# A head pair's two score matmuls start together, once both of their PSUM banks are free

## The chip, the cores and the metric

One core of one Trainium2 chip runs the whole program. The metric is the device time of one execution in microseconds, the median of several. Engine names are those of the profile: PE is TensorE's matmuls, PEld its weight loads, DVE VectorE, ACT ScalarE, POOL GpSimd, SP SyncE, which issues the DMAs.

## The reference

Sliding-window attention with sink tokens, and after it two feed-forward layers on its output:

```
scores = q @ k.T / sqrt(64);  keep = (key < n_sink) | (0 <= query - key < window)     # 4 sinks, window 128
a = softmax(where(keep, scores, -1e9));  x = a @ v                                    # batch 2, 8 heads, 768 tokens, 64 dims
x = relu(x @ w_in)**2 @ w_out                                                         # 1536 tokens, 512 -> 2048 -> 512
h = x @ w_in2;  out = (P(h) / Q(|h|)) @ w_out2                                        # rational function, P of degree 3, Q of degree 2
```

## The kernel before

**Attention** is cut into 24 steps: batch `bb` (2), block `j` of 256 queries (3), head pair `hp` (4). A step is `attention(bb, j, hp)` (L304). It takes two halves `qb` of 128 queries. In each half, both heads `hd` of the pair have one score matmul into a PSUM tile of their own, named `s{bb}_{j}_{hp}_{qb}{hd}`; in the rows of the order the batch is left out, so `s_2_0_10` is block 2, head pair 0, second half, first head. In batch 0 (`kl is None`) a head's q and k lie in 64 of the 128 partitions, head 0 in rows 0 to 63 and head 1 in rows 64 to 127, and a score is one f32 matmul at L329, which the hardware runs as two records. In batch 1 a head's operands are split into a high and a low part over 128 rows (L331, L332). I call the pair of the first half (`00`, `01`) pair a, and that of the second half (`10`, `11`) pair b.

After the scores, DVE merges the two key blocks under a predicate (L340), adds the mask and takes the row's minimum (L341), ACT takes the exponential (L348), DVE the reciprocal of the sum (L349, L350), POOL scales the row (L352). PE then transposes it into two more tiles, `pt` (L357, read by ACT at L365) and `sx` (L360, last read by DVE at L371), and multiplies with v into a tile `xo` (L382 to L386, last read by DVE at L390).

**The banks.** All these tiles come in turn from one pool of four PSUM banks: `ps_at = ... bufs=4, space=PSUM` (L186). A tile's first matmul waits until the tile that had its bank before has been read. The scheduler gives a tile the bank that comes free first, mostly that of the tile allocated four before. A step takes seven tiles: `s00 s01 s10 s11 pt sx xo`. Three steps are in flight (`att_pieces`, L491): the scores of step t, the transposes of step t-1, the output of step t-2. So four before pair a stand `s11` of step t-1 and `pt` of step t-2, and four before pair b stand `sx` of step t-2 and `xo` of step t-3. Where `xo` is read too late, `s11` takes the bank of its own step's `s00` instead: so in steps (1, 0) and (1, 1) among others.

**Beside it** runs the first feed-forward layer for the finished tokens (L400 into `h`, L439 into `acc`), and the decoding of its weights, which arrive as 64-bit words, in halves of 512 columns: ACT L63 and L65, DVE L66 and L67, ACT L299, POOL L300. The first 16 such halves are done while attention of batch 0 runs.

**The order** of each engine's queue is not that of the code. The framework's scheduler simulates the program and issues what is ready first, engine by engine (`schedule_with_timeline_sim=True`); on the chip every queue then runs strictly in that order.

Of the kernel before, what the change touches and what calls it, by code (L numbers as in the profile page):

```python
# [8 lines left out]
F32 = mybir.dt.float32  # L9
# [5 lines left out]
ALU = mybir.AluOpType  # L15
# [5 lines left out]
P = 128  # L21
# [5 lines left out]
SK = 32  # L27
# [13 lines left out]
def f32(ap):  # L41
    return ap.bitcast(F32)
# [133 lines left out]
def banded(ctx, tc, const, qk0, qk1, vb, vs, ns_f, win_f, wp, ab, scalars, out):  # L176
    nc = tc.nc
# [8 lines left out]
    ps_at = att_ctx.enter_context(tc.tile_pool(name="ps_at", bufs=4, space=PSUM))  # L186
    ps_a2 = att_ctx.enter_context(tc.tile_pool(name="ps_a2", bufs=2, space=PSUM))
    ac = att_ctx.enter_context(tc.tile_pool(name="ac", bufs=1))
    at = att_ctx.enter_context(tc.tile_pool(name="at", bufs=2))
# [4 lines left out]
    xh = [pers.tile([P, 4, 512], F32R, name=f"xh{g}", tag=f"xh{g}") for g in range(3)]  # L194
    xl = [pers.tile([P, 4, 512], F32R, name=f"xl{g}", tag=f"xl{g}") for g in range(3)]
# [105 lines left out]
        wh[L], wl[L] = h, lo  # L301


    def attention(bb, j, hp):  # L304

        n = f"{bb}_{j}_{hp}"
# [5 lines left out]
        e = at.tile([P, 2, 2 * W], F32, tag="e", name=f"e{n}")  # L312
        qk, kl, v = loaded[bb, j, hp]

        for qb in range(2):
            first = j == 0 and qb == 0
            nk = W if first else K0
            ss = []
            for hd in range(2):
                if hd == 0:  # L320
                    off = W * qb if j else 0
                else:
                    off = P if first else (W * (1 - qb) if j else 0)
                s = ps_at.tile([P, 512], F32, tag="at", name=f"s{n}_{qb}{hd}")
                cols = slice(qb * P, (qb + 1) * P)
                if kl is None:

                    rows = slice(hd * D, (hd + 1) * D)
                    nc.tensor.matmul(s[:, :nk], lhsT=qk[rows, cols], rhs=qk[rows, 256 + off : 256 + off + nk], start=True, stop=True)  # L329
                else:  # L330
                    nc.tensor.matmul(s[:, :nk], lhsT=qk[hd][:, cols], rhs=qk[hd][:, 256 + off : 256 + off + nk], start=True, stop=False)  # L331
                    nc.tensor.matmul(s[:, :nk], lhsT=qk[hd][:, cols], rhs=kl[hd][:, off : off + nk], start=False, stop=True)  # L332
                ss.append(s)
            for hd, s in enumerate(ss):
                u = 2 * qb + hd

                lo = 0 if hd == 0 or first else P
                if not first:
                    prev, own = (s[:, 0:P], s[:, W:K0]) if hd == 0 else (s[:, W:K0], s[:, 0:P])
                    nc.vector.copy_predicated(prev, own_u, own)  # L340
                nc.vector.tensor_tensor_reduce(  # L341
                    out=e[:, qb, hd * W : (hd + 1) * W], in0=s[:, lo : lo + W], in1=add[min(2 * j + qb, 2)][:, SK * (1 - hd) : SK * (1 - hd) + W],
                    scale=-SCALE, scalar=3.0e38, op0=ALU.add, op1=ALU.min, accum_out=nm[:, u : u + 1])
            c = slice(2 * qb, 2 * qb + 2)
            for hd in range(2):
                u = 2 * qb + hd
                eu = e[:, qb, hd * W : (hd + 1) * W]
                nc.scalar.activation(eu, eu, AF.Exp, bias=nm[:, u : u + 1], scale=-1.0, accum_out=sm[:, u : u + 1])  # L348
            nc.vector.tensor_scalar(out=rs[:, c], in0=sm[:, c], scalar1=GUARD, scalar2=None, op0=ALU.add)  # L349
            nc.vector.reciprocal(rs[:, c], rs[:, c])  # L350
            eq = e[:, qb, :].rearrange("p (h w) -> p h w", h=2)
            nc.gpsimd.tensor_tensor(out=eq, in0=eq, in1=rs[:, c].unsqueeze(2).to_broadcast([P, 2, W]), op=ALU.mult)  # L352
            yield
        pt = ps_at.tile([P, 4, P], F32, tag="at", name=f"pt{n}")
        for u in range(4):
            c0 = 0 if u < 2 else W + SK
            nc.tensor.matmul(pt[:, u, :], lhsT=e[:, u % 2, c0 : c0 + P], rhs=ident, is_transpose=True, start=True, stop=True)  # L357
        sx = ps_at.tile([P, 256], F32, tag="at", name=f"sx{n}")
        for qb in range(2):
            nc.tensor.matmul(sx[:, qb * P : (qb + 1) * P], lhsT=e[:, qb, P : 2 * P], rhs=ident, is_transpose=True, start=True, stop=True)  # L360

        pT = at.tile([P, 4, 2, P], F32, tag="pT", name=f"pT{n}", bufs=1)
        pa = at.tile([P, 4, P], F32, tag="pa", name=f"pa{n}", bufs=1)
        sT = at.tile([P, 256], F32R, tag="sT", name=f"sT{n}")
        nc.scalar.copy(pa, pt)  # L365
        nc.gpsimd.affine_select(out=pT[:, :, 1, :], in_=pa, pattern=[[0, 4], [1, P]], compare_op=ALU.is_ge, fill=0.0, base=0, channel_multiplier=-1)
        nc.gpsimd.affine_select(out=pT[:, :, 0, :], in_=pa, pattern=[[0, 4], [-1, P]], compare_op=ALU.is_gt, fill=0.0, base=0, channel_multiplier=1)

        half = slice(0, 2 * SK)
        nc.scalar.copy(sT[half], sx[half])  # L370
        nc.vector.tensor_tensor(out=sT[2 * SK :], in0=sx[half], in1=f32(sT[half]), op=ALU.subtract)  # L371
        yield
        xo = ps_at.tile([P, 256], F32, tag="at", name=f"xo{n}")
        pf = pT.rearrange("p (h q) o c -> p h (q o c)", q=2)
        nb = 2 if j == 0 else 3

# [10 lines left out]
        t0 = bb * S + j * 256  # L387
        g, c0 = t0 // 512, t0 % 512
        nc.scalar.copy(xh[g][:, hp, c0 : c0 + 256], xo)
        nc.vector.tensor_tensor(out=xl[g][:, hp, c0 : c0 + 256], in0=xo, in1=f32(xh[g][:, hp, c0 : c0 + 256]), op=ALU.subtract)  # L390
        yield


# [341 lines left out]
```

## Time and profile before

| | us |
|---|---|
| median of three runs | 660.72 (658.3 to 661.92) |
| the profiled execution | 661.41 |
| its span in the profile | 659.7 |
| PE busy | 638.3 (97%) |
| DVE, ACT, POOL busy | 464.2, 459.9, 400.1 |

Attention of batch 0, which the change touches, lies in the first 93 us; that of batch 1 ends before 200 us, and the rest is the feed-forward layers. A busy PE is not a PE at its best: two matmuls that run at the same time count once in its busy time, and at half clock a matmul counts twice as long.

### The profile page before, as it was taken

How to read it: one execution, taken by the hardware profiler on the slowest of the kernel's cores; microseconds unless marked ns; L12 is line 12 of the kernel's file. 1: busy time of each engine (PE TensorE's matmuls, PEld its weight loads, DVE VectorE, ACT ScalarE, POOL GpSimd, SP SyncE). 2: the span in 40 equal slices, each digit the busy share in tenths (PEclk: the TensorE clock that was granted, in tenths of full speed). 3: DMA queues.
4: the chain of work that ended last, by engine and by line, in shares of the span. 5: the costliest groups of instructions: out<-in, count | busy, mean ns of one | idle time of the engine just before them, and what ended most of it. 6: DMA issues, size and time to landing. Idle time of an engine off the chain costs nothing.

```text
span 659.7 us, 10180 instructions
## 1 busy us (share of the span) xinstructions
PE 638.3 (97%) x3376; PEld 523.5 (79%) x3376; DVE 464.2 (70%) x969; ACT 459.9 (70%) x938; POOL 400.1 (61%) x367
## 2 busy tenths in 40 slices
PE   5999999999999999999999999999999999999995
PEld 3567789999999887888888887878888888888883
DVE  7988977888823777737521489976699877676674
ACT  6877867767835767557432699977899776767771
POOL 4868867978735667556452789654666654444441
PEclk9979999999999999999999999999999999999998
DMA  7655553454001435304300042200020000001012
GB/s 246 199 172 166 167 165 94 127 131 128 26 13 38 155 128 178 142 28 163 128 1 0 19 140 66 96 1 0 22 106 33 1 0 1 0 1 64 1 64 70
DMA packets 25725, 54.16 MB, mean 82 GB/s; under 512 B 2880, under 2 KB 11072, under 8 KB 25664
## 3 DMA queue, kind: packets, MB, share of 16 engines
q1 hardware_dynamic: 25664, 53.43, 25.1%
q8 instruction: 29, 0.48, 0.3%
q14 instruction: 32, 0.26, 0.1%
HBM read 50.27 MB, written 3.15 MB: 81 GB/s over the span
## 4 chain that ended last, share of the span: by engine, by line
PE 72%; DVE 13%; ACT 7%; issue 3%; POOL 2%; DMA 1%; SPq 0%; DVEq 0%; ACTq 0%; POOLq 0%
PE h L400 31%; PE acc L441 16%; PE acc L439 15%; DVE wt L67 4%; PE xo L382 3%; DVE wr L66 3%; ACT sign L65 2%; PE s L329 2%; PE pt L357 2%; ACT wt L63 1%; POOL wl L300 1%; PE xo L385 1%; PE s L332 1%; DVE h L171 1%; PE s L331 1%
## 5 line engine op out<-in xcount | busy, mean ns | idle before, releaser
L164 POOL TENSOR_TENSOR z<-z,u 128x512 f32<-128x512 f32 x48 | 63.8, 1329 | 75.2 <-ACT z L163 75.0
L300 POOL TENSOR_TENSOR wl<-wt,wh 128x512 fp32r<-128x512 f32 x64 | 91.2, 1433 | 28.5 <-ACT wh L299 26.0
L409 POOL TENSOR_TENSOR gl<-sq,gh 128x256 fp32r<-128x256 f32 (+1 forms) x66 | 69.6, 1055 | 63.1 <-ACT gh L407 26.9
L409 POOL TENSOR_TENSOR gl<-z,gh 128x512 fp32r<-128x512 f32 x47 | 63.8, 1358 | 30.4 <-ACT gh L407 22.4
L66 DVE SCALAR_TENSOR_TENSOR wr<-wr,sign 128x512 uint32<-128x512 uint32 x64 | 60.3, 942 | 26.7 <-ACT sign L65 26.5
L130 DVE TENSOR_TENSOR sq<-sq,h 128x256 f32<-128x256 f32 (+1 forms) x66 | 35.5, 538 | 57.5 <-ACT sq L128 57.0
L67 DVE SCALAR_TENSOR_TENSOR wt<-wt,wr 128x512 uint32<-128x512 uint32 x64 | 67.4, 1053 | 3.6
L439 PE MATMUL acc<-gh,wh 128*128 128x256 f32 (+1 forms) x264 | 65.0, 334 | 1.2 <-ACT wh L299 1.2
L170 DVE SCALAR_TENSOR_TENSOR z<-z,con,h 128x512 f32<-128x512 f32 x48 | 35.7, 745 | 40.6 <-ACT h L169 36.6
L439 PE MATMUL acc<-gh,wl 128*128 128x256 f32 (+1 forms) x264 | 64.1, 332 | 0.0
L439 PE MATMUL acc<-gl,wh 128*128 128x256 f32 (+1 forms) x264 | 64.1, 335 | 0.0
L400 PE MATMUL h<-xh,wh 128*128 128x256 f32 (+1 forms) x264 | 61.3, 343 | 0.0
L441 PE MATMUL acc<-wh,gh 128*128 128x512 f32 x192 | 60.3, 393 | 0.1
L128 ACT ACTIVATE sq<-h 128x256 f32<-128x256 f32 (+1 forms) x66 | 31.4, 475 | 41.3 <-PE h L400 31.1
L441 PE MATMUL acc<-wl,gh 128*128 128x512 f32 x192 | 59.9, 391 | 0.0
L299 ACT CAST wh<-wt 128x512 fp32r<-128x512 f32 x64 | 39.3, 620 | 28.0 <-DVE wt L67 27.0
L400 PE MATMUL h<-xl,wh 128*128 128x256 f32 (+1 forms) x264 | 58.0, 336 | 0.0
L400 PE MATMUL h<-xh,wl 128*128 128x256 f32 (+1 forms) x264 | 57.4, 337 | 0.0
L441 PE MATMUL acc<-wh,gl 128*128 128x512 f32 x192 | 56.8, 390 | 0.0
L400 PE MATMUL h<-x2h,wh 128*128 128x512 f32 x192 | 53.8, 398 | 2.1 <-DVE z L172 2.1
L400 PE MATMUL h<-x2l,wh 128*128 128x512 f32 x192 | 53.6, 396 | 0.0
L400 PE MATMUL h<-x2h,wl 128*128 128x512 f32 x192 | 53.2, 396 | 0.0
(104 smaller groups left out, 1567.1 us busy)
## 6 DMA issues: line engine op xcount, KB each, us to landing
wr<-in_wp SPq DMA_DIRECT2D x64, 512.0 KB, 3.5
qkr<-in_qk SPq DMA_DIRECT2D x32, 176.0 KB, 3.1
v<-in_vb SPq DMA_DIRECT2D x16, 192.0 KB, 3.2
out<-accsb SPq DMA_DIRECT2D x12, 256.0 KB, 2.1
qkr<-in_qk SPq DMA_DIRECT2D x8, 352.0 KB, 3.9
qkr<-in_qk SPq DMA_DIRECT2D x16, 136.0 KB, 2.9
qkr<-in_qk SPq DMA_DIRECT2D x4, 272.0 KB, 4.9
v<-in_vb SPq DMA_DIRECT2D x8, 128.0 KB, 3.2
```

Source lines behind the costliest of these rows:

```text
L66: nc.vector.scalar_tensor_tensor(out=lo, in0=lo, scalar=29, in1=s, op0=ALU.logical_shift_right, op1=ALU.bitwise_or)
L67: nc.vector.scalar_tensor_tensor(out=t, in0=t, scalar=3, in1=lo, op0=ALU.logical_shift_left, op1=ALU.bitwise_or)
L128: nc.scalar.activation(r, h, AF.Relu)
L130: nc.vector.tensor_tensor(out=r, in0=r, in1=h, op=ALU.mult)
L164: nc.gpsimd.tensor_tensor(out=z, in0=z, in1=u, op=ALU.mult)
L170: nc.vector.scalar_tensor_tensor(out=z, in0=z, scalar=con[:, 2:3], in1=h, op0=ALU.add, op1=ALU.mult)
L299: nc.scalar.copy(h[:, c], t)
L300: nc.gpsimd.tensor_tensor(out=lo[:, c], in0=t, in1=f32(h[:, c]), op=ALU.subtract)
L400: nc.tensor.matmul(h[:, :n], lhsT=w_[:, k * P : (k + 1) * P], rhs=x_[:, k, c0 : c0 + n], start=p_ + k == 0, stop=p_ + k == 5)
L409: eng.tensor_tensor(out=gl[:, :n], in0=y, in1=f32(gh[:, :n]), op=ALU.subtract)
L439: nc.tensor.matmul(acc[m][:, :n], lhsT=w_[:, 512 + m * P : 512 + (m + 1) * P], rhs=g_[:, :n], start=st, stop=sp, skip_group_check=True)
L441: nc.tensor.matmul(acc[m], lhsT=g_[:, m * P : (m + 1) * P], rhs=w_[:, 512:1024], start=st, stop=sp)
```

## The change

In `attention`, both tiles of a half are allocated before its first matmul. A list `readers` notes the last reader of each tile of the pool, in the order of allocation. In batch 0 the first head's score matmul gets an explicit wait for the readers of both banks that the pair will take (the tiles three and four before), and the second head's matmul is tied by `keep_in_program_order` to its place behind the first. In batch 1 nothing is added.

```diff
+        def bank(shape, name):
+            readers.append(None)
+            return ps_at.tile(shape, F32, tag="at", name=name)
 ...
-            ss = []
-            for hd in range(2):
+            first_bank = len(readers)
+            tiles = [bank([P, 512], f"s{n}_{qb}{hd}") for hd in range(2)]
+            for hd, s in enumerate(tiles):
...
-                s = ps_at.tile([P, 512], F32, tag="at", name=f"s{n}_{qb}{hd}")
...
-                    nc.tensor.matmul(s[:, :nk], lhsT=qk[rows, cols], ...)
+                    mm = nc.tensor.matmul(s[:, :nk], lhsT=qk[rows, cols], ...)
+                    if hd:
+                        tc.keep_in_program_order(mm)
+                    elif first_bank >= 4:
+                        for r_ in readers[first_bank - 4 : first_bank - 2]:
+                            tc.add_manual_dep(mm.ins, r_.ins.name, mybir.DependencyInfo(mybir.DependencyClass.Sync, mybir.DependencyReason.DATA), reason="pair")
...
-                nc.vector.tensor_tensor_reduce(
+                readers[first_bank + hd] = nc.vector.tensor_tensor_reduce(
...
-        nc.scalar.copy(pa, pt)
+        readers[-2] = nc.scalar.copy(pa, pt)
...
-        nc.vector.tensor_tensor(out=sT[2 * SK :], ...)
+        readers[-1] = nc.vector.tensor_tensor(out=sT[2 * SK :], ...)
...
-        nc.vector.tensor_tensor(out=xl[g][:, hp, c0 : c0 + 256], ...)
+        readers[-1] = nc.vector.tensor_tensor(out=xl[g][:, hp, c0 : c0 + 256], ...)
```

The scheduler then makes another order on all engines for the first 95 us or so. On PE, in step (block 2, head pair 0), the queue before reads as follows (`h` and `acc` are the feed-forward layer's, the brackets name the queues that an instruction waits for):

```order
L329 MATMUL s_2_0_00_856<-qkr_2_0_721 128x288 [waits DMAHW1_49,DVE_49,PE_49]
L329 MATMUL s_2_0_01_858<-qkr_2_0_721 128x288 [waits Activation_49]
L329 MATMUL s_2_0_10_892<-qkr_2_0_721 128x288 [waits DVE_49]
L400 MATMUL h<-xh_97,wh_572 128x256 [waits DVE_49]
L400 MATMUL h<-xh_97,wh_572 128x256 x3
L400 MATMUL h<-xh_97,wl_573 128x256 x4
L400 MATMUL h<-xl_100,wh_572 128x256 x4
L439 MATMUL acc<-gh,wh_231 128x256 [waits Activation_49]
L439 MATMUL acc<-gh,wh_231 128x256 x3
L439 MATMUL acc<-gh,wl_232 128x256 x4
L329 MATMUL s_2_0_11_894<-qkr_2_0_721 128x288 [waits DVE_49,PE_49]
```

Here the second pair's two matmuls stand 20 feed-forward matmuls apart. The same step in the new queue:

```order
L452 MATMUL acc<-gh,wh_231 128x256
L337 MATMUL s_2_0_00_856<-qkr_2_0_721 128x288 [waits DMAHW2_49,Activation_49]
L337 MATMUL s_2_0_01_857<-qkr_2_0_721 128x288 [waits PE_49]
L452 MATMUL acc<-gh,wh_231 128x256 x2
L452 MATMUL acc<-gh,wl_232 128x256 x4
L452 MATMUL acc<-gl,wh_231 128x256 [waits Pool_49]
L452 MATMUL acc<-gl,wh_231 128x256 x3
L337 MATMUL s_2_0_10_892<-qkr_2_0_721 128x288 [waits DVE_49]
L337 MATMUL s_2_0_11_893<-qkr_2_0_721 128x288 [waits PE_49]
L413 MATMUL h<-xh_97,wh_572 128x256 [waits DVE_49]
```

Both pairs stand side by side now, and the feed-forward matmuls that had stood between the second pair's two stand around the pairs. Earlier, in step (block 1, head pair 2), PE's queue before has the first pair apart:

```order
L329 MATMUL s_1_2_00_539<-qkr_1_2_472 128x288 [waits DMAHW3_49,DVE_49,PE_49]
L357 MATMUL pt_1_0_506<-ident,e_1_0_420 128x128 [waits Pool_49]
L357 MATMUL pt_1_0_506<-ident,e_1_0_420 128x128 x2
L360 MATMUL sx_1_0_511<-ident,e_1_0_420 128x128
L400 MATMUL h<-xh_97,wh_191 128x256 [waits Activation_49]
L400 MATMUL h<-xh_97,wl_192 128x256 x4
L400 MATMUL h<-xl_100,wh_191 128x256 x3
L400 MATMUL h<-xh_97,wh_211 128x256
L400 MATMUL h<-xh_97,wl_212 128x256 x4
L400 MATMUL h<-xl_100,wh_211 128x256 x3
L329 MATMUL s_1_2_01_541<-qkr_1_2_472 128x288 [waits DVE_49,PE_49]
```

and the new one, where the transposes `pt_1_0` and `sx_1_0` have gone ahead of the output `xo_0_3`:

```order
L373 MATMUL sx_1_0_511<-ident,e_1_0_420 128x128
L395 MATMUL xo_0_3_522<-pT_0_3_455,v_0_3_301 64x256 [waits DMAHW4_49,DVE_49,PE_49]
L395 MATMUL xo_0_3_522<-pT_0_3_455,v_0_3_301 64x256
L395 MATMUL xo_0_3_522<-pT_0_3_455,v_0_3_301 64x128 x2
L398 MATMUL xo_0_3_522<-sT_0_3_457,vsh_109 128x256
L399 MATMUL xo_0_3_522<-sT_0_3_457,vsl_110 128x256
L337 MATMUL s_1_2_00_539<-qkr_1_2_472 128x288 [waits DMAHW3_49,DVE_49,Activation_49]
L337 MATMUL s_1_2_01_540<-qkr_1_2_472 128x288 [waits PE_49]
L413 MATMUL h<-xh_97,wh_191 128x256 [waits Activation_49]
L413 MATMUL h<-xh_97,wl_192 128x256 x4
```

The pair is whole and stands ahead of the long run of `h` matmuls. On DVE, the weight decoding (`wr`, `wt`) stands further forward among the attention steps. Before, between the second half of step (1, 1) and the first scores of step (1, 2):

```order
L66 SCALAR_TENSOR_TENSOR wr_0_554<-wr_0_554,sign_93 128x512
L341 ISA e_1_1_479,nm_1_1_476<-s_1_1_11_495,add_117 128x160
L341 ISA nm_1_1_476 128x1
L349 TENSOR_SCALAR rs_1_1_478<-sm_1_1_477 128x2
L67 SCALAR_TENSOR_TENSOR wt_0_556<-wt_0_556,wr_0_554 128x512
L350 RECIPROCAL rs_1_1_478<-rs_1_1_478 128x2
L349 TENSOR_SCALAR rs_1_1_478<-sm_1_1_477 128x2
L340 COPY_PREDICATED s_1_2_00_539<-own_u,s_1_2_00_539 128x128
```

and now:

```order
L67 SCALAR_TENSOR_TENSOR wt_1_565<-wt_1_565,wr_1_563 128x512
L363 RECIPROCAL rs_1_1_478<-rs_1_1_478 128x2
L354 ISA e_1_1_479,nm_1_1_476<-s_1_1_11_494,add_117 128x160
L354 ISA nm_1_1_476 128x1
L66 SCALAR_TENSOR_TENSOR wr_0_574<-wr_0_574,sign_93 128x512
L384 TENSOR_TENSOR sT_1_0_516<-sx_1_0_511,sT_1_0_516 64x256
L67 SCALAR_TENSOR_TENSOR wt_0_576<-wt_0_576,wr_0_574 128x512
L353 COPY_PREDICATED s_1_2_00_539<-own_u,s_1_2_00_539 128x128
```

The decoding is two halves further at this place (`wt_0_576` where `wt_0_556` stood; `wt_1_565` lies between them), and DVE's 16th half, the last of this stage, now comes before the end of step (2, 1) instead of step (2, 2).

## Rows read from the trace of the kernel before

**Rows 1.** The profile's page: busy time of each engine, PE's granted clock in 40 slices.
```profile
PE 638.3 (97%) x3376; PEld 523.5 (79%) x3376; DVE 464.2 (70%) x969; ACT 459.9 (70%) x938; POOL 400.1 (61%) x367
...
PEclk9979999999999999999999999999999999999998
```

**Rows 2.** Busy time by stretch; columns: stretch, its length, then engines, clock, DMA.
```profile
core 0: us, PE busy (x) PEld busy (x) DVE busy (x) ACT busy (x) POOL busy (x), PEclk, DMA share, GB/s
27.50:37.80 10.30, 8.73 (x48) 4.85 (x45) 10.00 (x37) 8.65 (x27) 8.79 (x10) 1.00 0.75 230
37.80:44.60 6.80, 6.80 (x28) 5.18 (x29) 4.62 (x14) 4.28 (x12) 3.71 (x5) 0.50 0.40 145
45.00:93.00 48.00, 47.19 (x333) 36.22 (x331) 41.76 (x133) 37.40 (x107) 37.55 (x42) 1.00 0.57 178
...
100.00:120.00 20.00, 20.00 (x175) 18.67 (x174) 14.76 (x53) 13.79 (x46) 14.85 (x21) 1.00 0.41 112
```

**Rows 3.** Timeline of PE from 50 us; columns: start, length, line, tiles, count, idle before.
```profile
50.91 0.76 PE L329 MATMUL s<-qkr 64*128 64x288 f32 x4
51.60 0.74 PE L439 MATMUL acc<-gh,wh 128*128 128x256 f32 x4
...
63.55 0.75 PE L329 MATMUL s<-qkr 64*128 64x288 f32 x2
64.23 0.66 PE L357 MATMUL pt<-ident,e 128*128 128x128 f32 x4
...
69.25 2.25 PE L329 MATMUL s<-qkr 64*128 64x288 f32 x6
71.43 0.74 PE L439 MATMUL acc<-gh,wh 128*128 128x256 f32 x4
...
80.26 0.72 PE L329 MATMUL s<-qkr 64*128 64x288 f32 x2 [0.56 <-DVE nm L341]
```

**Rows 4.** The score line's groups alone, between 45 and 93 us.
```profile
L329 PE MATMUL s<-qkr 64*128 64x288 f32 x46 | 12.4, 451 | 0.7 <-DVE nm L341 0.6
```

**Rows 5.** Timeline of PE before 45 us.
```profile
22.70 0.90 PE L329 MATMUL s<-qkr 64*128 64x160 f32 x2
23.53 0.58 PE L400 MATMUL h<-xh,wh 128*128 128x256 f32 x1
...
30.24 0.72 PE L329 MATMUL s<-qkr 64*128 64x288 f32 x2 [0.18 <-DVE rs L350]
...
34.54 1.49 PE L329 MATMUL s<-qkr 64*128 64x288 f32 x4 [0.67 <-DVE sT L371]
...
36.86 0.30 PE L357 MATMUL pt<-ident,e 128*128 128x128 f32 x1 [0.40 <-DVE xl L390]
...
39.96 1.33 PE L329 MATMUL s<-qkr 64*128 64x288 f32 x2
```

**Rows 6.** Timeline of DVE from 28 us, same columns.
```profile
28.01 0.42 DVE L371 TENSOR_TENSOR sT<-sx,sT 64x256 fp32r<-64x256 f32 x1
...
29.77 0.31 DVE L341 CUSTOM_DVE_ANT_0 e<-s,add 128x160 f32<-128x160 f32 x1
...
30.32 0.41 DVE L390 TENSOR_TENSOR xl<-xo,xh 128x256 fp32r<-128x256 f32 x1
...
36.31 0.41 DVE L390 TENSOR_TENSOR xl<-xo,xh 128x256 fp32r<-128x256 f32 x1
...
41.33 0.30 DVE L340 COPY_PREDICATED s<-own_u,s 128x128 f32<-128x128 uint32 x1 [1.69 <-PE s L329]
```

**Rows 7.** The chain that ended last, 53 to 81 us; columns: start, length, what.
```profile
53.03 1.72 POOL wl L300
...
67.94 1.68 DVE wt L67
...
80.26 0.72 PE s L329 x2
```

**Rows 8.** DVE's decoding groups between 45 and 93 us.
```profile
L67 DVE SCALAR_TENSOR_TENSOR wt<-wt,wr 128x512 uint32<-128x512 uint32 x9 | 9.3, 1036 | 0.1
...
L66 DVE SCALAR_TENSOR_TENSOR wr<-wr,sign 128x512 uint32<-128x512 uint32 x8 | 6.7, 833 | 1.7 <-ACT sign L65 1.7
```

More of the change, by code (lines that the diff above doesn't have):

```diff
@@ L301, in load_chunk @@
         wh[L], wl[L] = h, lo
+    readers = []
     def attention(bb, j, hp):
@@ L328, in attention @@
                     rows = slice(hd * D, (hd + 1) * D)
-                    nc.tensor.matmul(s[:, :nk], lhsT=qk[rows, cols], rhs=qk[rows, 256 + off : 256 + off + nk], start=True, stop=True)
+                    mm = nc.tensor.matmul(s[:, :nk], lhsT=qk[rows, cols], rhs=qk[rows, 256 + off : 256 + off + nk], start=True, stop=True)
+                    if hd:
[3 more added lines that the diff above has]
+                            tc.add_manual_dep(mm.ins, r_.ins.name, mybir.DependencyInfo(mybir.DependencyClass.Sync, mybir.DependencyReason.DATA), reason="pair")
                 else:
@@ L332, in attention @@
                     nc.tensor.matmul(s[:, :nk], lhsT=qk[hd][:, cols], rhs=kl[hd][:, off : off + nk], start=False, stop=True)
-                ss.append(s)
-            for hd, s in enumerate(ss):
+            for hd, s in enumerate(tiles):
                 u = 2 * qb + hd
@@ L353, in attention @@
             yield
-        pt = ps_at.tile([P, 4, P], F32, tag="at", name=f"pt{n}")
+        pt = bank([P, 4, P], f"pt{n}")
         for u in range(4):
@@ L357, in attention @@
             nc.tensor.matmul(pt[:, u, :], lhsT=e[:, u % 2, c0 : c0 + P], rhs=ident, is_transpose=True, start=True, stop=True)
-        sx = ps_at.tile([P, 256], F32, tag="at", name=f"sx{n}")
+        sx = bank([P, 256], f"sx{n}")
         for qb in range(2):
@@ L370, in attention @@
         nc.scalar.copy(sT[half], sx[half])
-        nc.vector.tensor_tensor(out=sT[2 * SK :], in0=sx[half], in1=f32(sT[half]), op=ALU.subtract)
+        readers[-1] = nc.vector.tensor_tensor(out=sT[2 * SK :], in0=sx[half], in1=f32(sT[half]), op=ALU.subtract)
         yield
-        xo = ps_at.tile([P, 256], F32, tag="at", name=f"xo{n}")
+        xo = bank([P, 256], f"xo{n}")
         pf = pT.rearrange("p (h q) o c -> p h (q o c)", q=2)
@@ L389, in attention @@
         nc.scalar.copy(xh[g][:, hp, c0 : c0 + 256], xo)
-        nc.vector.tensor_tensor(out=xl[g][:, hp, c0 : c0 + 256], in0=xo, in1=f32(xh[g][:, hp, c0 : c0 + 256]), op=ALU.subtract)
+        readers[-1] = nc.vector.tensor_tensor(out=xl[g][:, hp, c0 : c0 + 256], in0=xo, in1=f32(xh[g][:, hp, c0 : c0 + 256]), op=ALU.subtract)
         yield
```

## The prediction

> **What bounds the kernel now.** I read the page's busy times first, then busy time by stretch, then PE's timeline in the stretch that the change touches, and last the chain of waits. PE is busy for 97% of the span, the next engine for 70% [rows 1]. From 100 us on PE has no idle time at all in a 20 us stretch, while DVE is at 14.76 of 20 [rows 2]. So what PE has less to do before 93 us should arrive at the end nearly whole, if PE then finds its operands ready. That "if" is the whole question, for before 93 us the others are close behind: between 45 and 93 us PE is busy 47.19 of 48 us, but DVE 41.76, POOL 37.55 and ACT 37.40; between 27.5 and 37.8 us DVE is the fullest engine, with 10.00 of 10.3 [rows 2]. And the chain of waits leaves PE for a while: it runs over POOL's decoding at 53 us and DVE's at 68 us, and is on a score at 80.26 [rows 7]. PE is full there, but does not set the pace alone.
>
> **What a pair costs, together and apart.** A pair whose two matmuls stand side by side, four records, begins at 50.91 and the next work at 51.60: 0.69 us. One alone, two records, begins at 63.55, the next work at 64.23: 0.68 us [rows 3]. So the second head is free when it starts with the first, and a pair that is split costs twice. In the run of six records at 69.25 three matmuls came one by one, as their banks came free, and took 2.18 us to the next work at 71.43 [rows 3]. The change cannot shorten a matmul; it can only let two run in the time of one.
>
> **The change part by part.**
>
> *Scores after 45 us.* There are 46 records there, 12.4 us of busy time [rows 4]: 23 matmuls, the second of pair a in step (1, 2) and all that come after it. In the new order that first one has moved to its partner before 45 us, and the other 22 form 11 pairs with nothing between them. Eleven times 0.76 us, the busy time of a pair [rows 3], is 8.4 us. PE loses 12.4 - 8.4 = 4.0 us of work. The stretch runs at full clock (1.00) and has 0.8 us of idle time [rows 2], so this is worth 4.0 us if nothing else gets late.
>
> *Scores before 45 us.* Here the pairs b of steps (1, 0) and (1, 1) are split by their banks, and the new wait shows what it does. In step (1, 0) the first matmul could start once `sx` was read, at 28.43, and the second started at 30.24, after its bank's reader at 29.77 [rows 5, 6]. Now both wait for the reader of `xo` as well, which runs from 30.32 to 30.73 [rows 6]: the pair ends 0.5 us later than its second matmul did. In step (1, 1) the two started one after the other from 34.54 on [rows 5]; the reader of `xo` is done at 36.72 [rows 6]. With 0.69 us for the pair the next work starts at 37.4, where the transpose after it began at 36.86 (it waited for that same reader) [rows 5]: 0.5 us later. The two `h` matmuls that followed the pair now stand ahead of it and fill some of the wait. The bounds are nothing, since DVE has other work while it waits and the new order gives it decoding, and, with nothing covered, 0.5 us and the 1.4 us by which the second matmul of step (1, 1) is held (36.72, against a start at 34.54 + 1.49 - 0.72 = 35.31): 1.9 us. I take 0.5 + 0.5 = 1.0 us. Pair a of step (0, 3) is whole now too and frees 0.83 us of PE, 22.70 to 23.53 [rows 5]; I don't count it, since what follows waits for DVE.
>
> *New waits after 45 us.* A first score that waits holds up everything behind it in PE's queue: the feed-forward matmuls, which need no bank of this pool, and the transposes that ACT and POOL wait for. The new order answers this by placing pairs later, behind feed-forward matmuls. The bounds are nothing and the whole 4.0 us. The nearest rows are the waits of this line in the split order: one of 0.56 us after 45 us, one of 0.67 us before [rows 3, 5]. I take one more of that size, 0.6 us, for all pairs together.
>
> *DVE's load.* If the stretch shrinks from 48 to 44 us with the same work, DVE would be busy 41.76 / 44 = 95%, hardly without new waits. But two halves of decoding have moved ahead, 1.04 + 0.83 = 1.87 us each [rows 8], to where DVE idles: between 37.8 and 44.6 us it is busy 4.62 of 6.8 [rows 2], with one wait of 1.69 us for a score [rows 6]. So 41.76 - 3.74 = 38.0 us are left for 44, 86%, against 87% now. I count nothing for it.
>
> *Sum.* -4.0 + 1.0 + 0.6 = -2.4 us. The profiled execution took 661.41 us, 0.7 us above the median of the three runs; from it the sum gives 659.0, and against the median of 660.72, which I forecast, 658.3 us.
>
> *A rule that speaks against it.* The row first: the scores are read by DVE, and DVE is busy for 97% of the stretch from 27.5 to 37.8 us, PE for 85% [rows 2]. The Trainium skill, TensorEngine Tiling (Array Packing), section PSUM Bottleneck, says that array packing speeds up TensorE but not the emptying of PSUM, which may then become the bottleneck. Before 45 us the trace agrees with it, and the sum counts no gain there; by the rule alone the 4.0 us after 45 us would be gone too, which is the second rival.
>
> **The rivals.**
>
> 1. *All of it arrives, and the clock too.* Between 37.8 and 44.6 us PE ran at a granted clock of 0.50, 1.2 GHz, after a stretch with idle time (8.73 busy of 10.3) [rows 2]; a score alone takes 1.33 us there against 0.75 [rows 3, 5]. PE is full in that stretch, so it costs 3.4 us. If the new order fills PE's queue better just before, that stretch goes or gets short: with no new wait either, -4.0 - 3.4 = -7.4 us, 653.3 us; without the clock, but with pair (0, 3), -4.8 us, 655.9 us. For it: the transposes and the whole pair now stand ahead of the `h` matmuls in step (1, 2). Against it: two matmuls in the time of one leave PE less to do just before 37.8 us, not more.
>
> 2. *Emptying PSUM and decoding set the pace.* The chain over POOL and DVE [rows 7] ends as late as before, and PE's saving turns into idle time: 660.7 us, or up to 1 us less. For it: those rows. Against it: the two halves that have moved ahead.
>
> 3. *The other side: the clock.* A pair that holds the queue makes PE idle, and idle time is what preceded the stretch at 0.50. One mechanism: the waits at the banks of pairs b between 28 and 60 us grow long enough that a second such stretch follows. It costs 3.4 us, and it decides from the point where the waits have eaten the savings, that is with 4.0 us of new idle time. Then 660.7 + 0.6 + 3.4 = 664.7 us. For it: PE's idle time from 27.5 to 37.8 us is 1.57 us already, and a slot of 0.72 us at 30.24 [rows 5] joins it. Against it: after 45 us PE's longest wait is 0.56 us and the clock stays at 1.00. The Trainium skill, TensorE: Matmul & The Clock Gate, section on psum-queue depth-cycling, describes it: small idle times between groups of matmuls that cycle through PSUM banks make the clock go back and forth. The one stretch at 0.50 here fits that; by the rule more waits at banks mean more such stretches, which is this rival's time.
>
> 4. *It doesn't do what it says.* The pairs stand together in the queue but start apart. The four records at 50.91 speak against that; the early waits alone would then cost their 1.0 us: 661.7 us.
>
> **How the numbers follow.** A measurement of this kernel can tell about 0.5% from no change, 3.3 us: below 657.4 us is faster, above 664.0 slower. My forecast, 656.6 to 660.0 around 658.3, has 0.43; some 0.15 of that lies below 657.4. Rival 1 has 0.22, all faster. Rival 2 has 0.18, all within. Rival 3 has 0.13, nearly all slower; rival 4 has 0.04, within. That is faster 0.37, same 0.51, slower 0.12. The range leaves out the far end of rival 1 and the upper half of rival 3: 654.4 to 663.8 us. The likeliest case by itself is 656.6 to 660.0.
>
> **What would show it.** The scores' busy time after 45 us falls from 12.4 to about 8.4 us, in runs of four records of 0.76 us (rival 4 if not). All of batch 0's scores are done 2 to 3 us earlier. If they are not, and PE idles for 3 to 4 us before them with POOL or DVE as releasers, rival 2 was right. The page's clock shows whether the stretch at 0.50 stays (forecast), goes (rival 1) or is doubled (rival 3). From 200 us on every group must take the same time as now; a difference there would mean that the reordering carries further than I saw, through the DMAs of the weights above all.

## The result, and the profile after

The changed kernel takes 667.14 us (median of 6, 666.87 to 667.84) against 660.61 us before (median of 6, 658.3 to 662.42): a ratio of 1.0121, 95% interval 1.0099 to 1.0143. It is slower by 1.2% or 6.5 us, where I had forecast 658.3 us and a range that ended at 663.8. The profiled execution took 667.68 us, with a span of 666.0. In its page, the busy times and PE's granted clock in slices, which answer to [rows 1]:

```profile
PE 633.4 (95%) x3376; PEld 519.6 (78%) x3376; DVE 463.1 (70%) x969; ACT 459.9 (69%) x938; POOL 399.2 (60%) x367
...
PEclk9979999999999999999999999999999999999999
```

PE has 4.9 us less to do (638.3 before) and the span is 6.3 us longer, so PE idles some 11 us more. Where, the busy times by stretch show, cut at the same two events in both kernels: the start of the output `xo` of step (1, 0) and the end of attention of batch 0. Before:

```profile
4.62:48.04 43.42, 38.37 (x156) 23.61 (x157) 39.23 (x145) 33.90 (x100) 30.44 (x31) 0.92 0.64 214
48.04:93.00 44.96, 44.29 (x316) 34.57 (x316) 39.45 (x125) 34.77 (x101) 35.42 (x40) 1.00 0.58 180
```

and after, with the stretch that answers to the last of [rows 2]:

```profile
4.67:53.06 48.39, 35.74 (x156) 21.54 (x156) 39.95 (x147) 36.16 (x105) 31.06 (x33) 0.89 0.61 204
53.06:98.66 45.60, 42.16 (x318) 32.89 (x317) 37.15 (x121) 32.32 (x97) 32.80 (x38) 1.00 0.52 161
100.00:120.00 20.00, 20.00 (x178) 18.94 (x175) 13.31 (x54) 13.51 (x43) 13.61 (x20) 1.00 0.35 95
```

In the first stretch PE's idle time goes from 5.05 to 12.65 us; its work shrinks by 2.6 us, so the stretch is 5.0 us longer. In the second, 2.1 us less work meet 2.8 us more idle time: the saving is gone, and 0.6 us with it. By lag I mean, here and below, how much later PE starts the matmul record of the same number than in the kernel before. From 100 us on it is constant at 5.7 us, but for 1.0 us more at one wait for a half of weights (1.23 us at 255 us before, 2.26 at 262 after), against the forecast that every group takes the same time from 200 us on. Nearly all of the loss is made in the first 53 us, and the gain is lost after it. PE's timeline there (answering to [rows 5]):

```profile
33.04 0.76 PE L337 MATMUL s<-qkr 64*128 64x288 f32 x4 [0.86 <-DVE xl L403]
...
36.19 0.87 PE L395 MATMUL xo<-pT,v 128*64 128x256 f32 x8 [1.58 <-issue]
...
40.12 0.76 PE L337 MATMUL s<-qkr 64*128 64x288 f32 x4 [1.51 <-DVE xl L403]
...
45.45 1.33 PE L337 MATMUL s<-qkr 64*128 64x288 f32 x4 [1.34 <-ACT pa L378]
```

Every pair runs as four records in the time of one: 0.76 us, or 1.33 at half clock. But pair b of steps (1, 0) and (1, 1) waits for the reader of an output (0.86 and 1.51 us), pair a of step (1, 2) for that of `pt` (1.34 us). In between PE waits 1.58 us. The profile names no releaser for it; by the order of allocation it is for the bank of a score of step (1, 0), and PE goes on when DVE has read that score, late, in the gaps that weight decoding (L66, L67) leaves:

```profile
33.05 1.73 DVE L66 SCALAR_TENSOR_TENSOR wr<-wr,sign 128x512 uint32<-128x512 uint32 x1
34.70 0.28 DVE L353 COPY_PREDICATED s<-own_u,s 128x128 f32<-128x128 uint32 x1
...
34.97 0.68 DVE L67 SCALAR_TENSOR_TENSOR wt<-wt,wr 128x512 uint32<-128x512 uint32 x1
35.57 0.28 DVE L353 COPY_PREDICATED s<-own_u,s 128x128 f32<-128x128 uint32 x1
35.77 0.31 DVE L354 CUSTOM_DVE_ANT_0 e<-s,add 128x160 f32<-128x160 f32 x1
```

The chain that ended last (answering to [rows 7]) leaves PE here for POOL and ACT (decoding and softmax), and comes back to it at 46.91 us:

```profile
34.62 1.57 issue
36.19 0.89 PE xo L395 x8
...
38.78 1.75 POOL wl L300
...
44.97 0.43 ACT pa L378
...
46.91 3.79 PE h L413 x16
```

The granted clock falls too: PE is idle for 4 of the 10.3 us ahead of the stretch at 0.50 (1.2 GHz), and the stretch is 10.2 us long, not 6.8:

```profile
31.60:41.90 10.30, 6.33 (x42) 3.75 (x41) 8.45 (x33) 6.62 (x18) 6.73 (x8) 1.00 0.60 201
41.90:52.10 10.20, 8.73 (x36) 5.92 (x36) 7.03 (x21) 8.05 (x23) 7.08 (x7) 0.50 0.52 161
```

### The profile page after: what moved, and what is told of

Read it like the earlier page. It is cut to its first block, busy times and chain, and to the rows that moved or that the text cites. A ratio compares the mean times of both kernels' runs of the same rounds, so it can differ in the third digit from the quotient of the medians.

```text
span 666.0 us, 10176 instructions
## 1 busy us (share of the span) xinstructions
PE 633.4 (95%) x3376; PEld 519.6 (78%) x3376; DVE 463.1 (70%) x969; ACT 459.9 (69%) x938; POOL 399.2 (60%) x367
## 4 chain that ended last, share of the span: by engine, by line
PE 70%; DVE 12%; ACT 9%; issue 3%; DMA 2%; POOL 2%; SPq 1%; DVEq 0%; ACTq 0%; POOLq 0%
PE h L413 31%; PE acc L454 15%; PE acc L452 14%; DVE wt L67 4%; DVE wr L66 3%; PE xo L395 3%; ACT sign L65 2%; ACT wt L63 2%; PE pt L370 1%; ACT e L361 1%; PE s L337 1%; POOL wl L300 1%; DMA wr<-in_wp 1%; PE s L346 1%; DVE h L171 1%
## 5 line engine op out<-in xcount | busy, mean ns | idle before, releaser
L66 DVE SCALAR_TENSOR_TENSOR wr<-wr,sign 128x512 uint32<-128x512 uint32 x64 | 61.5, 962 | 28.3 <-ACT sign L65 28.1
L67 DVE SCALAR_TENSOR_TENSOR wt<-wt,wr 128x512 uint32<-128x512 uint32 x64 | 67.4, 1053 | 4.3 <-DVE wr L66 0.5
L128 ACT ACTIVATE sq<-h 128x256 f32<-128x256 f32 (+1 forms) x66 | 31.4, 476 | 42.0 <-PE h L413 31.8
L365 POOL TENSOR_TENSOR e<-e,rs 128x320 f32<-128x320 f32 x48 | 35.7, 746 | 30.1 <-DVE rs L363 21.1
```

The lines of the kernel that those rows point to most:

```text
L66: nc.vector.scalar_tensor_tensor(out=lo, in0=lo, scalar=29, in1=s, op0=ALU.logical_shift_right, op1=ALU.bitwise_or)
L67: nc.vector.scalar_tensor_tensor(out=t, in0=t, scalar=3, in1=lo, op0=ALU.logical_shift_left, op1=ALU.bitwise_or)
```

## The experiments

My first theory (A) was that pairs held for their banks in the first six steps make the loss. The rivals: waits after 45 us (B, D), or the new order itself. In the run late below, the first six steps have the joint allocation but neither wait nor pin, and PE starts its matmuls there as before (lag 0.1 us up to 25 us); no run has the pin alone.

**The wait at some pairs alone.** Four kernels, each the changed one with a condition on the step or the half. Their names are late, early, pair_a and pair_b, and what I expected of them follows in that order:

```diff
+                    paired = 4 * j + hp >= 6       # late; early: < 6; pair_a: qb == 0; pair_b: qb == 1
-                    if hd:
+                    if hd and paired:
...
-                    elif first_bank >= 4:
+                    elif not hd and paired and first_bank >= 4:
```

> The explicit wait and the pin stand only from step (1, 2) of batch 0 on; the six steps before it are issued as in the kernel before, so PE's queue is that of the kernel before up to its first matmul of step (1, 2), at about 40 us. Theory A (the loss is made by the pairs held in the first six steps, where four banks and the softmax of one step set the pace): the time is 657 to 661.5 us, no lag before 40 us, and the stretch at clock 0.50 stays at about 6.8 us from 37.8 us on. Theory B (the savings after 45 us turn into waits at the banks, and these waits cost as much again): 662 to 665 us, with a lag that grows between 45 and 95 us. Theory C (the wait at a weight chunk near 255 us is set off by any shorter stretch of pairs): another 1.0 us is lost at 255 us, whatever went before.

> The explicit wait and the pin stand only in the first six steps of batch 0, (0, 0) to (1, 1). Theory A: 664 to 668 us, since all of the loss is kept, with a lag of about 5 us at 50 us; what the later pairs would have saved is not saved either. Theory B: 661 to 663 us, as the lost time of the later pairs is missing.

> The explicit wait and the pin stand only at the pairs of the first half of a step (a). Theory A1 (the loss begins with the pair a of step (0, 2), held from 11.9 to 14.65 us, and each later hold adds to it): a lag of 2 us or more at 20 us and a time of 663 to 666 us. Theory A2 (only the pairs b, which wait for the output tile three steps back, cost time): 658 to 661.5 us and no lag above 0.5 us at 20 us.

> The explicit wait and the pin stand only at the pairs of the second half of a step (b). Theory A1: 661 to 664 us, a part of the loss, from the pairs b of steps (1, 0) and (1, 1) alone. Theory A2: 665 to 668 us, all of it.

Measured: late 662.03 us (1.0029, 1.0005 to 1.0052), early 664.75 (1.0081, 1.0052 to 1.0111), pair_a 664.26 (1.007, 1.0044 to 1.0097), pair_b 672.81 (1.0217, 1.017 to 1.0265). Half of the waits cost more than all of them: the parts don't add up, as each kernel gets another order from the scheduler. Late has a lag of -3.7 us at 54 us, that is, it is ahead of the kernel before, without any stretch at 0.50 after the clock's first rise; by 76 us it is 1.1 us behind. PE's waits between 42 and 100 us in it (who waits for whom: us in all, times, longest):

```profile
PE h L414 <- DVE sq L130: 4.7, 5, 1.6
```

The feed-forward matmuls that were to fill in wait for DVE. That speaks for D.

**Six banks for the first six steps**, the second pairs on the accumulators' pool, which is empty until then. The expectations are those of the changed kernel with six banks (six_after) and of the kernel before with them (six_before):

```diff
+            six = bb == 0 and qb == 1 and 4 * j + hp < 6
+                tiles = [ps_a2.tile([P, 512], F32, tag="acc", name=f"s{n}_{qb}{hd}") for hd in range(2)]
```

> The changed kernel, but the second pairs of the first six steps of batch 0 take their two banks from the pool of the accumulators, which stands empty until the first acc matmul: six banks instead of four for these steps, and the explicit wait of such a pair is for the second pair of the step before. Hold theory (the loss is made by pairs that wait for a bank in the first six steps): the waits for xl and sT before 45 us go, the lag at 50 us falls from 5 to about 1 us, and the time is 659 to 663 us. Order theory (the loss is made by the order that the scheduler gives, whichever bank is waited for): 664 us or more.

> The kernel before with the same six banks for the first six steps and no explicit wait. Hold theory: the kernel before has few bank waits there (0.7 us for sT, 0.4 us for xl), so 658 to 661 us. Order theory: it can fall anywhere between 657 and 668 us, since every change to the program gives another order.

Measured: 667.39 us (1.0072, 1.0049 to 1.0095) and 664.9 (1.0051, 1.0025 to 1.0078). Two more banks help neither. Six_after has no lag at 30 us (3.3 in the changed kernel) and 5.7 us at 40, and its clock stands at 0.50 for 20.5 us, from 31.8 on. Theory A is in doubt, and the order, which changed here too, is not ruled out.

**Less decoding on DVE, with the order left to the scheduler**, in the kernel before (before_light) and in late (late_light):

```diff
+    light = n.split("_")[0] in list("01234567")
+    if not light:
         nc.vector.scalar_tensor_tensor(out=lo, in0=lo, scalar=29, in1=s, ...)
```

> The kernel before without DVE's first decoding operation (the one that puts sign and low bits together, L66) for the first 16 halves of weights, so that these weights lose their three lowest bits: 16 x 0.83 = 13.3 us less on DVE before 95 us. Theory D (between 45 and 93 us the emptying of PSUM and the decoding on DVE set the pace, not PE): the time falls by 2 us or more, to 658 us or less. Theory P (PE sets the pace there, as forecast): within 1 us of the kernel before.

> The kernel with wait and pin from step (1, 2) on (run late), and the same decoding operation left out for the first 16 halves. Theory D: with DVE relieved PE no longer waits 4.7 us for DVE's product (sq) of the feed-forward layer, so the saved matmul time arrives: 3 to 6 us below the kernel before with the same omission. Theory B (banks and the latency of one step hold PE back, not DVE's load): not faster than the kernel before with the same omission, as late was not faster than before.

Measured: 656.77 us (0.9906, 0.9882 to 0.993) and 664.89 (1.0032, 0.9997 to 1.0067). The first is what theory D expected, the second what theory B did. Neither decides, as both had new orders. From here on I fixed the order.

**Fixed queues.** Each engine's queue is given as a table, and each instruction gets an edge of order, without a semaphore, behind the one ahead of it in the table. The framework then issues exactly that order. (In these kernels the scores are at L434, their reads at L446, `sT` at L476, `xo` at L487, `xh` and `xl` at L494 and L495, `h` at L505.) The three expectations below are for the new queues without the wait (new_queues_no_wait), the old queues with six pairs joined (joined_late), and with all nine (joined).

```diff
+    for e, q in table.items():
+        for a, b in zip(q, q[1:]):
+            tc.add_manual_dep(t[b], t[a].name, mybir.DependencyInfo(mybir.DependencyClass.NoSync, ...), reason="queue")
```

> The kernel before, with the queues of all five engines fixed, instruction by instruction, to those of the changed kernel (and the same banks), but without the explicit wait: a pair's first matmul waits for its own bank alone, its second for its own. Order theory (the loss comes from the order that the scheduler makes with the wait in its simulation): 665 to 668 us, within 1.5 us of the changed kernel. Hold theory (the loss is the time by which the first score is held for the second one's bank): 662 us or less, as the first head's softmax starts 0.5 to 1.5 us earlier at each pair with late banks.

> The kernel before with its own queues on all engines, fixed instruction by instruction, but for six moves on PE: in the six split pairs from step (1, 2) on the first head's matmul is moved down to stand right ahead of the second. No explicit wait. Order theory: PE saves 6 x 0.68 = 4.1 us of matmul time and nothing else is moved, so 656 to 659 us, unless Theory D (DVE and POOL pace the stretch) holds, by which the saving turns into idle time: 660 to 662 us, with PE idle 3 to 4 us more between 45 and 95 us. Hold theory: the first scores that are read later make DVE late: 661 to 664 us.

> As the run before it, with all nine split pairs of batch 0 joined, the three before step (1, 2) too: (0, 2) a, (0, 3) a and (1, 0) b. Order theory: like the run with six, 655 to 660 us. Hold theory: the three early ones cost 0.5 us or more each, 1 to 3 us above the run with six.

The new queues without the wait take 667.62 us (1.0126, 1.0093 to 1.0159): all of the loss. So the loss comes with the new order, not with the explicit wait. PE has the same bank wait, 2.0 us now, and the first stretch up to the same event is nearly as long as in the changed kernel (47.63 us against 48.39):

```profile
PE xo L487 <- issue: 2.0, 1, 2.0
```

```profile
4.67:52.30 47.63, 40.20 (x156) 24.61 (x156) 40.46 (x147) 36.15 (x104) 31.01 (x33) 0.89 0.63 207
```

Starting the first score early keeps PE busy (40.20 against 35.74 us), but a single then runs at a pair's price, and what follows is 0.8 us sooner, no more. The counterpart, the old queues with the wait, was not tried: in step (1, 2) the first score would wait for the read of `pt`, whose transposes stand behind it in the queue.

The old queues with six pairs joined take 662.64 us (1.0052, 1.0031 to 1.0074), with nine 662.71 (1.0051, 1.0031 to 1.0072). The three early pairs cost nothing, against what the hold theory expected of them. Of the six late ones one does the harm, step (1, 2) a, moved down 20 places, behind 16 `h` matmuls (the run without this move, joined5, shows it below). PE's timeline in the run with six:

```profile
42.94 0.76 PE L434 MATMUL s<-qkr 64*128 64x288 f32 x4
44.46 0.50 PE L505 MATMUL h<-xl,wh 128*128 128x256 f32 x2 [0.77 <-DVE xl L495]
44.90 0.76 PE L434 MATMUL s<-qkr 64*128 64x288 f32 x4
47.77 0.86 PE L462 MATMUL pt<-ident,e 128*128 128x128 f32 x4 [2.12 <-DVE sT L476]
```

The first score comes 3 us later than before (39.96, [rows 5]); DVE, whose queue it heads, is late with all that is behind it, and PE idles 2.12 us: at this one pair the hold theory was right. The stretch at 0.50 ends sooner than before, and a second one follows, of the same length in sum:

```profile
37.80:41.20 3.40, 3.37 (x17) 2.73 (x18) 1.91 (x7) 2.63 (x8) 1.02 (x2) 0.50 0.31 113
48.00:51.40 3.40, 3.40 (x20) 2.31 (x19) 3.08 (x13) 3.40 (x11) 1.73 (x3) 0.50 0.79 256
```

The next four, all with fixed queues, are the old queues with five pairs joined (joined5), the old queues with less decoding (old_light), both together (joined5_light), and the new queues with DVE's decoding moved back (new_dve_back).

> As the run with six moves on PE (the kernel before, own queues, no explicit wait), but without the move of step (1, 2) a, which stood 20 matmuls higher: only the five split pairs from step (2, 0) b on are joined, all after 58 us. Theory D (DVE, ACT and the transfers pace the stretch after 45 us, so saved matmul time turns into waits): 659 to 662 us, within 1 us of the kernel before, PE idle 2 to 3 us more after 58 us. Theory P (PE sets the pace there): 5 x 0.68 = 3.4 us faster, 656 to 658 us.

> The kernel before with its own queues fixed on all engines; left out is DVE's first decoding operation (L66) for the first 16 halves of weights, so that these lose their three lowest bits, 13.3 us less on DVE before 95 us and no other instruction moved. Theory D: 2 to 5 us faster than the kernel before, as PE's waits for DVE before 45 us and after go. Theory P: within 1 us of it.

> The same omission, and the five late pairs joined on PE. Theory D: with DVE relieved the joined pairs bring what they save, 2 to 3.4 us below the run with the omission alone. If something else than DVE's load takes the saving (a transfer, the latency of one step through four engines): within 1 us of that run.

> The queues of the changed kernel without the explicit wait (as in the run that kept all its queues), but on DVE the decoding operations of nine halves of weights before 45 us stand behind the reads of PSUM that they stood ahead of or between (scores, sT, xl). All other queues are those of the changed kernel. DVE-order theory (the decoding that the scheduler put ahead on DVE makes scores and banks late, and PE idle): 3 us or more of the 6.5 come back, 661 to 664.5 us. If PE's own order before 45 us makes the loss (pairs behind the transposes and the output of the steps before): 666 us or more.

Joined5 takes 660.47 us (1.0002, 0.9973 to 1.0032): no change. Up to 58 us its lag is 0.1 us or less, so fixing the queues costs nothing by itself. Its score group between 58 and 93 us and PE's waits there stand below the same group of before:

```profile
L329 PE MATMUL s<-qkr 64*128 64x288 f32 x32 | 9.3, 450 | 0.7 <-DVE nm L341 0.6
```

```profile
L434 PE MATMUL s<-qkr 64*128 64x288 f32 x32 | 6.8, 453 | 0.7 <-DVE sT L476 0.7
```

```profile
PE s L434 <- DVE sT L476: 0.7, 1, 0.7
PE h L505 <- ACT xh L494: 0.6, 1, 0.6
PE pt L462 <- DVE nm L446: 0.3, 1, 0.3
```

2.5 us of matmul time are saved and 1.0 us of new waits stand against them. In this execution 1.2 us arrive (its lag goes from -0.1 us at 58 us to -1.3 at 100); in the median nothing does. Old_light takes 653.76 us (0.9904, 0.9871 to 0.9937), joined5_light 652.65 (0.9885, 0.9848 to 0.9922). So work taken from DVE, with no instruction moved, gives 6.4 us, where joining pairs gives nothing. (The 13.3 us of the expectation are 16 times the mean of [rows 8]; in the trace of the kernel before these 16 operations take 15.1 us, and DVE's busy time falls by 17.6 us, 464.2 to 446.6.) But the joined pairs bring only 1.1 of their 3.4 us even then, with intervals that overlap, and in the two profiled executions 1.0 us between 45 and 100 us, no more than in joined5. Theory D's reason for the lost pairs, DVE's load, is not borne out. Nor is most of the gain made in D's stage: by 45 us old_light is 4.5 us ahead, and 1.6 us are added after that. Busy time from 20 to 40 us, before and in old_light:

```profile
20.00:40.00 20.00, 18.43 (x81) 10.97 (x81) 19.24 (x63) 16.36 (x47) 15.59 (x17) 0.94 0.59 185
```

```profile
20.00:40.00 20.00, 19.44 (x95) 12.06 (x94) 15.02 (x63) 17.62 (x51) 14.53 (x18) 1.00 0.65 209
```

DVE is full before, with 19.24 of 20 us. Relieved, it lets PE go from 18.43 to 19.44, and the stretch at 0.50 does not come at all. By an estimate that alone is 3.4 of the 4.5 us, half of 6.8, as PE was busy for all of that stretch [rows 2].

New_dve_back, which puts the decoding behind the reads of PSUM on DVE alone, takes 674.72 us (1.0219, 1.0181 to 1.0257), 6 us by the ratios and 7 by the medians worse than with the queues as they were. ACT's queue, which I had left, shows why, and under it PE's:

```profile
38.98 0.62 ACT L404 CAST wh<-wt 128x512 fp32r<-128x512 f32 x1 [2.25 <-DVE wt L67]
```

```profile
41.35 0.80 PE L505 MATMUL h<-xh,wh 128*128 128x256 f32 x2 [2.85 <-ACT xh L494]
```

On ACT the copy of the weights stands ahead of the softmax and of `xh`; it waits 2.25 us for the decoding that now comes later, and PE waits for what is behind it. So this run does not tell whether decoding moved ahead on DVE is the harm: what it added on ACT covers that. One queue can't be changed without the others.

The last three are the new queues with less decoding (new_light), the old queues without an addition on DVE (old_noguard), and the same with five pairs joined (joined5_noguard).

> All queues of the changed kernel, fixed, without the explicit wait, and DVE's first decoding operation (L66) left out for the first 16 halves of weights, which lose their three lowest bits. Load theory (the new order costs time because DVE, full before 45 us, is made to wait and cannot make it up): with 13.3 us less on DVE most of the loss goes, 652 to 657 us, within 3 us of the old queues with the same omission (653.8). Path theory (PE's pairs stand behind transposes and output in the queue, so scores come later whatever DVE does): 5 us or more of the loss stay, 659 us or more.

> The kernel before with its queues fixed, but the softmax's reciprocal is taken of the sum itself: the addition of 1e-9 to the sum on DVE (L349, 48 instructions of 128x2) is left out, which changes nothing in f32 since the largest term of each sum is 1. Between 4.6 and 45 us 12 of them take 5.7 us on DVE. Load theory (DVE paces the first 45 us): 2 to 5 us faster, 655 to 658 us. If their time is only time in which DVE would have waited anyway: within 1 us of the kernel before.

> The same without the addition, and the five late pairs joined on PE. Load theory: 0.5 to 2 us below the run without the joining, as with the decoding operation left out (1.1 us); if DVE is not relieved enough after 58 us: the same time.

New_light takes 658.57 us (0.9957, 0.993 to 0.9983). With less on DVE the new queues cost 0.5% more than the old ones, 4.8 us by the medians, where they cost 1.3% with all of it. That is between the two theories. The traces tell where: at 100 us the new queues are 1.7 us behind the old ones with less decoding, and 4.9 us with all of it. So in the attention of batch 0 most of the loss hangs on a full DVE. The other 2.6 us come at the wait for weights that costs the changed kernel 1.0 us too: PE waits 2.3 us for ACT's `wh` (1.2 in old_light), and a stretch at 0.50 follows.

```profile
253.00:256.40 3.40, 3.40 (x10) 2.62 (x9) 3.40 (x6) 2.57 (x5) 1.94 (x2) 0.50 0.30 110
```

In the attention PE still waits 1.2 us for that bank and 1.1 us for `xo`. These are one profiled execution each.

Old_noguard takes 657.14 us (0.994, 0.9911 to 0.9968) and joined5_noguard 656.85 (0.9932, 0.9903 to 0.9961), both faster than either kernel. The edit, and the group that it removes in the kernel before, between 4 and 45 us:

```diff
-            nc.vector.tensor_scalar(out=rs[:, c], in0=sm[:, c], scalar1=GUARD, scalar2=None, op0=ALU.add)
-            nc.vector.reciprocal(rs[:, c], rs[:, c])
+            nc.vector.reciprocal(rs[:, c], sm[:, c])
```

```profile
L349 DVE TENSOR_SCALAR rs<-sm 128x2 f32<-128x2 f32 x12 | 5.7, 479 | 0.5 <-ACT e L348 0.4
```

3.7 us come from leaving out 48 tiny instructions on the engine that is full. Joining the pairs adds 0.3 us to that, which is no difference. Both omissions also shorten a chain by one operation, that of the weights and that of the softmax; no run tells this apart from DVE's load.

**The clock in these times.** The 91 executions of the kernel before that ran beside the experiments fall into two groups: 31 with a mean granted clock of 0.995 or more, median 658.3 us, and 60 with 0.993 or less, median 661.6. The 3.3 us between them are about what the stretch at 0.50 costs (half of 6.8), but of the first group there is no trace. All executions of old_light are at 0.997 or more, and eight of nine of old_noguard at 0.994 or more. Against the kernel before in its first group beside them (657.9 and 658.1 us) 4.1 us are left of the 6.4, and for those eight 1.1 of the 3.7: the rest goes with the clock. Split in the same way, joined5 is 1.1 us faster than before in the first group (2 against 6 executions) and 0.5 in the second (8 against 8). The new queues without the wait are at 0.980 to 0.990, and 6.4 us slower than the second group beside them (661.2), so the groups do not make this part of the loss.

## Why the prediction was wrong, step by step

I forecast -2.4 us, and it came to +6.5. Two steps failed by 4 us each: the gain of 4.0 us after 45 us, taken as time saved because PE was nearly full there, and the +1.0 us before 45 us, which came to +5.0 because the new order was read as mere filling. A third, smaller one is the 1.0 us at the weights near 260 us, for which the sum had nothing.

*Scores after 45 us* (-4.0): the work went as I said. The group that answers to [rows 4] has two more records (pair a of step (1, 2) came at 45.45 us, later than I had placed it), and two of its pairs ran at half clock, yet it takes 2.2 us less. The pairs run together, so rival 4 is out:

```profile
L337 PE MATMUL s<-qkr 64*128 64x288 f32 x48 | 10.2, 506 | 1.6 <-ACT pa L378 1.3 <-DVE xl L403 0.2
```

What failed is "this is worth 4.0 us if nothing else gets late". I took a stretch in which PE is busy for 98% as one in which PE sets the time. Joined5 is that step alone for five pairs: of 2.5 us saved nothing arrives in the median, 1.2 us in the profiled execution. PE's new waits there, 0.7, 0.6 and 0.3 us, are all for reads of PSUM (`sx`, `xo` and a score). The Trainium skill, TensorEngine Tiling (Array Packing), section PSUM Bottleneck, which I had weighed as a rule against the change, says that the emptying of PSUM may become the bottleneck. The trace agrees beyond 45 us too: the scores' 9.3 us became 6.8, and the time stayed (1.0002).

*Scores before 45 us* (+1.0): mis-sized by 4 us, and for the wrong reason. I priced the hold of two pairs, and in the new order the hold costs nothing that can be measured: without it the new queues take 667.6 us. The step failed in pricing the wait and not the order that the scheduler makes with it, which I had shown at three places and read as filling.

*New waits after 45 us* (+0.6): they came to 2.8 us more idle time between 53 and 99 us.

*DVE's load* (0): I averaged it over 48 us and counted nothing. DVE was the fullest engine from 27.5 to 37.8 us [rows 2], and this is the row that should have led: taking work from it moves the time by 3.7 and 6.4 us, a good part of it through the clock, while saving PE's work moves it by some 1 us at most. With less on DVE the new order loses 1.7 us by 100 us, not 4.9. Whether it is the decoding moved ahead that does the harm, as I then thought, stays open, as the run that put it back on DVE alone made ACT wait.

*The rivals.* Rival 3 came closest, 664.7 us with a chance of 0.13, in part by luck: the waits did eat the savings, and the time at half clock grew, by 3.4 us of stretch and by a later first rise (27.5 to 31.6 us; before it a pair takes 1.33 us, though the column PEclk reads 1.00 there). But its cause was wrong, since the loss stays when the wait goes. The new idle time came to 12.65 - 5.05 = 7.6 us in the first stretch, not 4.0; without the wait it is 47.63 - 40.20 = 7.4 us in all, and singles at a pair's price take the rest. Nor does the clock make up the loss, though it is worth some 3 us to the kernel before: the six executions of the changed kernel have mean granted clocks from 0.981 to 0.990 and times within 1 us, while those of the kernel before beside the run of the new queues go from 659.1 to 662.4 us at 0.988 to 0.993 and from 656.7 to 659.5 at 0.995 to 0.998. At 0.988 to 0.990, where the two meet, it is 666.9 to 667.8 us against 661.5 to 662.4. Rival 2 was right on the second half.

*Open:* which instruction of the new order does most of the harm. The bank wait at 36 us and the pairs behind the transposes are seen, but no run took one of them alone out of the new queues. Nor is it known why the wait near 260 us grows with the new order: it does so in the changed kernel, in the new queues without the wait and in new_light (2.3 us each), and not in late or joined5 (1.2). What takes the rest of the joined pairs' saving after 45 us, with DVE relieved or not, is open beyond the three waits shown.

## What to carry to other kernels

An edge that is added for one engine is an input to the scheduler for all of them: price the order that comes out, engine by engine, or fix the queues and change one thing in them. A share of 98% for PE does not make PE the bound; ask which engine is full in the stretch whose results the others wait for, and try to take work from that one. Then split the executions by their granted clock before a gain is put down to the work itself. Where queues run in order, moving an instruction on one engine costs whatever stands behind its consumers on the next.

## What the runs showed of the hardware

How long some operations take on DVE depends on what POOL does. Before 45 us the addition to 128x2 elements took 479 ns on average, the reciprocal of the same shape 158 ns (12 in 1.9 us). Over the whole kernel before (shortest, median and longest in ns) the addition varies sevenfold and the reciprocal hardly:

```profile
L349 DVE TENSOR_SCALAR rs<-sm x48: 142/170/1115, 9.4 to 181.6; 128x2 f32<-128x2 f32 x48
```

```profile
L350 DVE RECIPROCAL rs<-rs x48: 152/165/168, 10.0 to 181.8; 128x2 f32<-128x2 f32 x48
```

DVE's additions in the changed kernel with an operation of the decoding, and POOL beside them:

```profile
30.50 0.64 DVE L362 TENSOR_SCALAR rs<-sm 128x2 f32<-128x2 f32 x1
...
34.90 0.15 DVE L362 TENSOR_SCALAR rs<-sm 128x2 f32<-128x2 f32 x1
...
37.01 0.69 DVE L66 SCALAR_TENSOR_TENSOR wr<-wr,sign 128x512 uint32<-128x512 uint32 x1 [0.17 <-ACT sign L65]
```

```profile
29.90 0.63 POOL L379 TENSOR_SCALAR_AFFINE_SELECT pT<-pa 128x512 f32<-128x512 f32 x1 [0.43 <-PE xo L395]
30.48 0.63 POOL L380 TENSOR_SCALAR_AFFINE_SELECT pT<-pa 128x512 f32<-128x512 f32 x1
...
32.96 1.27 POOL L300 TENSOR_TENSOR wl<-wt,wh 128x512 fp32r<-128x512 f32 x1
36.31 0.72 POOL L365 TENSOR_TENSOR e<-e,rs 128x320 f32<-128x320 f32 x1 [2.08 <-ACT wh L299]
37.22 0.97 POOL L379 TENSOR_SCALAR_AFFINE_SELECT pT<-pa 128x512 f32<-128x512 f32 x1 [0.20 <-PE xo L395]
```

The addition that starts with a POOL operation ends with it, 0.64 us; the one at 34.90, with POOL idle, takes 0.15. L66 takes 1.73 us at 33.05 beside `wl`, and its fellow L67 0.68 at 34.97 with POOL idle. In these cases the one that starts second pays: L66 at 37.01 takes 0.69 us, and the POOL operation that begins beside it at 37.22 takes 0.97 us, where the one of the same line at 29.90 took 0.63. The Trainium skill, GPSIMD Engine Reference, section Key points, says that the two engines share their way into SBUF and that DVE's operations with two SBUF inputs, or in a mode of two ports, contend with GpSimd. The times of the decoding, with two inputs, agree with it; whether the addition, with one, runs in such a mode no trace here shows. And old_light, old_noguard and the two joined kernels built on them, four of the fastest, have this in common: after the clock's first rise, at 27.2 to 29.3 us, PE is never at 0.50 again before the end. Late shows the same and gains nothing by it.
